# When TensorE reads the weight offsets of its blocks into registers

## The chip, the cores and the metric

The kernel runs on one core of one Trainium2 chip. The metric is the device time of one execution in microseconds (us), the median of several runs. A core has five engines that work side by side: TensorE (PE in the profile, with its weight loads shown apart as PEld), VectorE (DVE), ScalarE (ACT), GpSimd (POOL) and SyncE (SP), which here only issues DMA transfers. Each engine has a sequencer that takes its instructions in order, and a letter q behind the engine's name in the profile (PEldq, SPq) means an instruction of the sequencer.

## What is computed

An attention layer that picks chunks of keys, and behind it a mixture of experts. The second half is what matters here:

```python
def reference(**kwargs):
    attn_out = _attn_ref(q, k, v)                 # (4, 8, 768, 64)
    x = attn_out.transpose(0, 2, 1, 3).reshape(3072, 512)
    return _moe_ref(x, ...)

def _moe_ref(x, w_gate, w1_dense, w2_dense, w1, w2):
    h_dense = np.maximum(x @ w1_dense, 0.0)       # dense path, every token
    y_dense = h_dense @ w2_dense
    logits = x @ w_gate                           # 8 experts
    expert_idx = np.argmax(logits, axis=1)        # one expert for a token
    ...                                           # gate_w: its softmax weight
    for e in range(E):
        mask = expert_idx == e
        h = np.maximum(x[mask] @ w1[e], 0.0)
        y_moe[mask] = gate_w[mask, None] * (h @ w2[e])
    return y_dense + y_moe
```

Which tokens an expert gets is known only on the chip. So the kernel sorts the tokens by expert into a table in DRAM, and works through it in 31 blocks of 128 rows (24 full blocks' worth of tokens, and up to 7 more because each expert's last block may be partly filled). Each block belongs to one expert.

## The kernel before

There are 16 pairs of heads in four batches; a batch's gate, ranks and dense path are filled in between the attention work of the next batch. The last batch has no next one: its dense path lies between the first blocks of experts. All weights of the experts are in SBUF, in one tile. What tells one block's expert from another's is an offset along the columns of this tile. VectorE works the offsets out in two lists, one of the first N1 = 11 blocks, known before the last batch is routed, and one of the other N2 = 20. They are whole numbers in a row of one partition, `eo`; a second row `ro` says where a block's rows begin in the table.

```python
    N1 = (N * (B - 1) // B - E * 127 + 127) // 128
    N2 = NBLK - N1
...
    eo = const.tile([1, NBLK], mybir.dt.int32)
    ro = const.tile([1, NBLK], mybir.dt.int32)
    zo = const.tile([1, E], mybir.dt.int32)
...
        def lists(last, cnt):
            def row(name, n=E, dt=FP):
                return mg.tile([1, n], dt, name=f"{name}{last}", bufs=1)
            I32 = mybir.dt.int32
            n, i0 = (N2, N1) if last else (N1, 0)
            ...
            nc.vector.tensor_reduce(out=ef, in_=ge, op=ALU.add, axis=mybir.AxisListType.X)
            nc.vector.tensor_scalar(eo[:, i0 : i0 + n], ef, float(E - 1), float(2 * NK * 512), ALU.min, ALU.mult)
```

TensorE needs an offset in a register of its sequencer. The helper `registers` makes one read instruction for all values of a slice; `load_offs(n)` reads those up to block n that haven't been read yet. SyncE reads `ro` in the same way.

```python
    offs = []
    rows = []

    def registers(to, src, engine, n, top, why):
        k = len(to)
        _, v = nc.values_load_multi_w_load_instructions(src[:, k:n], engines=[engine], min_val=0, max_val=top,
                                                        skip_runtime_bounds_check_because=why)
        to.extend(v)

    def load_offs(n):
        registers(offs, eo, mybir.EngineType.PE, n, (E - 1) * 2 * NK * 512, "the expert of a block is at most the last")

    def load_rows(n):
        registers(rows, ro, mybir.EngineType.SP, n, EMPTY, "blocks lie in their expert's rows, or are the empty one")
```

In the last pair of heads, SyncE reads its first list and starts to fetch the first blocks' rows:

```python
            if p == NP - 1 and u == 5:
                load_rows(N1)
            if p == NP - 1 and u >= 5:
                fetch(u - 5)
```

Then come the blocks. `tx` transposes a block's rows on TensorE, VectorE copies them out of PSUM. `e1` is the first matmul with the expert's weights (four instructions, each at the block's offset plus a constant), ScalarE applies the relu. `th` transposes the result, ScalarE copies it. `e2` is the second matmul, VectorE multiplies by the token's gate weight, and GpSimd adds the rows to the output by an indirect DMA.

```python
        wef = we.rearrange("p e j f -> p (e j f)")
        def tx(i):
            s = es[i]
            tp = p1.tile([128, NK, 128], HF, name="tp", tag="tr")
            for ko in range(NK):
                nc.tensor.transpose(tp[:, ko], s["x"][:, ko * 128 : (ko + 1) * 128].bitcast(HF), ident)
            s["xT"] = xT = et.tile([128, NK, 128], HF, name="exT")
            nc.vector.tensor_copy(xT, tp)
...
        def e1(i):
            s = es[i]
            hp = p2.tile([128, 512], FP, name="hp", tag="h")
            for ko in range(NK):
                nc.tensor.matmul(hp, s["xT"][:, ko], wef[:, bass.ds(offs[i] + ko * 512, 512)],
                                 start=(ko == 0), stop=(ko == NK - 1))
            s["h"] = h = et.tile([128, 512], HF, name="eh")
            nc.scalar.activation(h, hp, AF.Relu)

        def th(i):
            s = es[i]
            tp = p1.tile([128, NK, 128], HF, name="tp", tag="tr")
            for j in range(NK):
                nc.tensor.transpose(tp[:, j], s["h"][:, j * 128 : (j + 1) * 128], ident)
            s["hT"] = hT = et.tile([128, NK, 128], HF, name="ehT")
            nc.scalar.copy(hT, tp)
...
        def e2(i):
            s = es[i]
            yp = p3.tile([128, Dm], FP, name="yp", tag="y")
            for j in range(NK):
                nc.tensor.matmul(yp, s["hT"][:, j], wef[:, bass.ds(offs[i] + (NK + j) * 512, 512)],
                                 start=(j == 0), stop=(j == NK - 1))
            o = et.tile([128, Dm], FP, name="yo", bufs=4)
            nc.vector.tensor_scalar(o, yp, s["x"][:, Dm : Dm + 2].bitcast(FP), None, ALU.mult)
            sc = nc.gpsimd.indirect_dma_start(
                out=out, out_offset=bass.IndirectOffsetOnAxis(ap=s["x"][:, Dm + 2 : Dm + 4].bitcast(mybir.dt.int32), axis=0),
                in_=o, in_offset=None, bounds_check=N - 1, oob_is_err=False, compute_op=ALU.add)
            apart(sc, "add", "every token is in one block")
```

The loop puts `e1` of a block, the transposes of the next, parts of the last batch's dense path (`extra`), `e2` of the block before and `th` of this one behind each other:

```python
        AHEAD = 8
        READY = 3
        load_offs(N1)
        tx(0)
        extra = {0: a[:NT] + [a[NT], ranks], 1: places, 2: [empty]}
        for n, f in enumerate(d):
            extra.setdefault(1 + n * (N1 - 2) // len(d), []).append(f)
        got = FIRST
        for i in range(NBLK):
            if i == READY:
                load_rows(NBLK)
            if i + 1 == N1:
                load_offs(NBLK)
            while got < min(i + AHEAD + 1, NBLK if i >= READY else N1):
                fetch(got)
                got += 1
            e1(i)
            if i + 1 < NBLK:
                tx(i + 1)
            for f in extra.get(i, ()):
                f()
            if i > 0:
                e2(i - 1)
            th(i)
        e2(NBLK - 1)
```

`load_offs(N1)` stands ahead of the first block, `load_offs(NBLK)` at the head of block 10.

Of the kernel before, what the change touches and what calls it, by code (L numbers as in the profile page):

```python
# [12 lines left out]
ALU = mybir.AluOpType  # L13
# [4 lines left out]
def kernel(  # L18
# [12 lines left out]
    nc = tc.nc  # L31
# [4 lines left out]
    E = 8  # L36
    F = 512
    NK = Dm // 128
# [4 lines left out]
    NBLK = NM + E - 1  # L43
# [3 lines left out]
    const = ctx.enter_context(tc.tile_pool(name="const", bufs=1))  # L47
# [5 lines left out]
    EMPTY = E * CAP  # L53
# [3 lines left out]
    N1 = (N * (B - 1) // B - E * 127 + 127) // 128  # L57
    N2 = NBLK - N1
# [100 lines left out]
    num = const.tile([128, NM, 1], mybir.dt.int32)  # L159
    zt = const.tile([128, XW], U16)  # L160
    used = const.tile([1, E + 1], FP)
    eo = const.tile([1, NBLK], mybir.dt.int32)
    ro = const.tile([1, NBLK], mybir.dt.int32)
    zo = const.tile([1, E], mybir.dt.int32)
    xbig = [const.tile([128, NT, XW], HF, name=f"xbig{i}") for i in range(2)]
# [87 lines left out]
    def batch_fills(b):  # L253
# [63 lines left out]
# [7 lines that stand above are left out]
            nb = row("nb", dt=I32)  # L324
            nc.vector.tensor_single_scalar(nb, cnt, 127.0 if last else 0.0, ALU.add)
            nc.vector.tensor_single_scalar(nb, nb, 7, ALU.arith_shift_right)
            nf = row("nf")
            if last:
                nc.vector.tensor_tensor(nf, nb, used[:, 0:E], ALU.subtract)  # L329
                nc.vector.tensor_tensor(zo, cnt, erow, ALU.add)  # L330
            else:
                nc.vector.tensor_copy(nf, nb)
            cum = row("cum")
            nc.vector.tensor_tensor_scan(cum, eone, nf, 0.0, ALU.mult, ALU.add)
            step = row("step")
            if last:
                nc.vector.tensor_tensor(step, used[:, 1 : E + 1], used[:, 0:E], ALU.subtract)
                nc.vector.tensor_tensor(step, step, nf, ALU.subtract)
                nc.vector.tensor_scalar(step, step, 128.0, float(CAP), ALU.mult, ALU.add)
            else:  # L340
                nc.vector.tensor_scalar(step, nf, -128.0, float(CAP), ALU.mult, ALU.add)
                left = row("left")
                nc.vector.tensor_tensor(left, nf, cum, ALU.subtract)
                nc.vector.tensor_single_scalar(left, left, float(N1), ALU.add)
                nc.vector.scalar_tensor_tensor(used[:, 0:E], left, 0.0, nf, ALU.max, ALU.min)
            ge = mg.tile([1, n, E], FP, name=f"ge{last}", bufs=1)
            nc.vector.tensor_tensor(ge, iob[:, 0:n].unsqueeze(2).to_broadcast([1, n, E]),
                                    cum.unsqueeze(1).to_broadcast([1, n, E]), ALU.is_ge)
            ef = row("ef", n)
            nc.vector.tensor_reduce(out=ef, in_=ge, op=ALU.add, axis=mybir.AxisListType.X)  # L350
            nc.vector.tensor_scalar(eo[:, i0 : i0 + n], ef, float(E - 1), float(2 * NK * 512), ALU.min, ALU.mult)
            nc.vector.tensor_tensor(ge, ge, step.unsqueeze(1).to_broadcast([1, n, E]), ALU.mult)
            rs = row("rs", n)
            nc.vector.tensor_reduce(out=rs, in_=ge, op=ALU.add, axis=mybir.AxisListType.X)
            nc.vector.scalar_tensor_tensor(rs, iob[:, 0:n], 128.0, rs, ALU.mult, ALU.add)
            if last:
                h0 = row("h0", 1)
                nc.vector.tensor_single_scalar(h0, used[:, 0:1], 128.0, ALU.mult)
                nc.vector.tensor_scalar(ro[:, i0 : i0 + n], rs, h0, float(EMPTY), ALU.add, ALU.min)
            else:  # L360
                nc.vector.tensor_copy(ro[:, 0:n], rs)
# [52 lines left out]
        at = {}  # L414
# [10 lines left out]
    offs = []  # L425
    rows = []

    def registers(to, src, engine, n, top, why):
        k = len(to)
        _, v = nc.values_load_multi_w_load_instructions(src[:, k:n], engines=[engine], min_val=0, max_val=top,  # L430
                                                        skip_runtime_bounds_check_because=why)
        to.extend(v)

    def load_offs(n):
        registers(offs, eo, mybir.EngineType.PE, n, (E - 1) * 2 * NK * 512, "the expert of a block is at most the last")

    def load_rows(n):
        registers(rows, ro, mybir.EngineType.SP, n, EMPTY, "blocks lie in their expert's rows, or are the empty one")

    es = [dict() for _ in range(NBLK)]  # L440

# [7 lines left out]
    with (  # L449
# [38 lines left out]
        def prep_kt(p):  # L488
            kp = st[p]["kp"]
            nc.vector.tensor_copy(kT[p % NB][0][0:64], kp[0:64])  # L490
            nc.vector.tensor_copy(kT[p % NB][1][64:128], kp[64:128])
# [121 lines left out]
        for i, (p, u) in enumerate(seq):  # L613
            n1 = p + 1 if p + 1 < NP else None
            n2 = p + 2 if p + 2 < NP else None
            if i + ahead_n < len(seq):
                scores(*seq[i + ahead_n])
            if u == 2 and n1 is not None:
                prep_s(n1)
            if u == 4 and n2 is not None:  # L620
                prep_k(n2)
            if u == 5 and n2 is not None:
                prep_q(n2)
            if u == 7 and n2 is not None:
                prep_kt(n2)
            if u == 9 and n2 is not None:
                prep_ub(n2)
            for f in fills.pop(i % (HP * NU) - LAG, ()):
                f()
            if i >= LAG:  # L630
                finish(*seq[i - LAG])
            if u == 0 and n2 is not None:
                cast_v(n2)
                load(p + 4, "v")
                if p == 1:
                    load_dense(st[n2]["cast"])
                if p == 2:
                    route_consts()
                for _ in range(2 if p >= 10 else 1):
                    if p > 1 and wq:  # L640
                        load_expert(*wq.pop(0), st[n2]["cast"])
            if u == 7:
                cast_qk(p + 3)
                load(p + 5, "kq")
            if p == NP - 1 and u == 5:
                load_rows(N1)
            if p == NP - 1 and u >= 5:
                fetch(u - 5)
        for i in range(len(seq) - LAG, len(seq)):
# [4 lines left out]
    with (  # L654
# [8 lines left out]
        a, d, ranks, places, _ = batch_fills(B - 1)  # L663
# [19 lines left out]
# [20 lines that stand above are left out]
            if i < N1:  # L703
                tc.declare_no_dep(sc.ins, group="dense", reason="the first blocks hold no token of the last batch")
                tc.add_to_no_dep_group("add1", sc.ins)
# [10 lines left out]

        AHEAD = 8
        READY = 3
        load_offs(N1)
        tx(0)  # L720
        extra = {0: a[:NT] + [a[NT], ranks], 1: places, 2: [empty]}
        for n, f in enumerate(d):
# [2 lines left out]
        for i in range(NBLK):  # L725
            if i == READY:
                load_rows(NBLK)
            if i + 1 == N1:
                load_offs(NBLK)
            while got < min(i + AHEAD + 1, NBLK if i >= READY else N1):  # L730
                fetch(got)
                got += 1
# [4 lines that stand above are left out]
                f()  # L737
            if i > 0:
                e2(i - 1)
            th(i)  # L740
        e2(NBLK - 1)

# [29 lines left out]
```

## Time and profile before

| | |
|---|---|
| device time, median of 3 runs | 298.36 us (296.98 to 298.44) |
| span of the profiled execution | 296.6 us |
| mean granted TensorE clock | 0.947 |
| TensorE busy | 232.7 us, 78% of the span |
| VectorE / ScalarE / GpSimd busy | 64% / 59% / 55% |
| attention ends, first transposes of a block | 188.8 us |
| first matmul of block 0 / of block 30 | 192.53 / 287.12 us |
| last scatter issued | 292.3 us |

The page has the span in 40 slices of 7.4 us; each digit is the busy share in tenths, PEclk the granted clock of TensorE in tenths:

```profile
PE   1179777797499988499998499598599819999991
PEclk9999999999789999989999989979799977999997
DMA  7999999989497999399999237404769981786781
```

The blocks of experts fill about the last 14 digits. In the row of TensorE there are dips at every batch's end, and a "1" among the blocks of experts. In a list of groups, a row has line, engine, operation, the tiles written and read, the count, the busy time and the mean of one in ns, and behind a second bar the idle time of the engine just before these instructions with what ended it. Reads into registers aren't counted as busy time; they show as idle time of the engine, or in a view of the tile that they read.

### The profile page before, as it was taken

Reading aid. Unit: us, or ns where it says so; the run is one execution under the profiler, and the core shown is the slowest. Engines: PE = TensorE matmul, PEld = TensorE weight load, DVE = VectorE, ACT = ScalarE, POOL = GpSimd, SP = SyncE. Lnnn points to the kernel's source line nnn. Section 1 sums busy time; section 2 is a strip of 40 time slices with the busy share of each in tenths; the row PEclk is TensorE's granted clock in tenths of the full one; section 3 lists DMA queues with packets and bytes.
Section 4 is the critical chain, followed back from the end, with each engine's and each line's share of the span. In section 5 each row is a group of like instructions: output and inputs, shape, how many; then the busy total and the mean of one; then the engine's idle time right before and its main releaser. Section 6 shows DMA issues by size and latency. Waiting matters only on the chain.

```text
span 296.6 us, 7417 instructions
## 1 busy us (share of the span) xinstructions
PE 232.7 (78%) x2595; PEld 151.9 (51%) x2595; DVE 189.0 (64%) x592; ACT 174.2 (59%) x325; POOL 162.5 (55%) x200
## 2 busy tenths in 40 slices
PE   1179777797499988499998499598599819999991
PEld 1056555575267666266676266364255405555550
DVE  6479899999368899469799652354343503555542
ACT  3639788875269996359895359333255403555550
POOL 7575855665645664845665522007644413767674
PEclk9999999999789999989999989979799977999997
DMA  7999999989497999399999237404769981786781
GB/s 196 272 256 229 161 237 217 221 226 194 151 169 210 249 215 225 120 189 194 178 232 196 96 94 198 106 2 173 161 110 218 240 175 20 123 155 105 97 123 14
DMA packets 75972, 50.04 MB, mean 169 GB/s; under 512 B 30112, under 2 KB 69024, under 8 KB 75936
## 3 DMA queue, kind: packets, MB, share of 16 engines
q1 hardware_dynamic: 60288, 30.58, 40.8%
q0 software_dynamic: 15648, 18.99, 39.4%
q8 instruction: 21, 0.34, 0.5%
q14 instruction: 15, 0.12, 0.1%
HBM read 41.96 MB, written 18.88 MB: 205 GB/s over the span
## 4 chain that ended last, share of the span: by engine, by line
PE 24%; issue 24%; POOL 19%; ACT 10%; DVE 9%; DMA 6%; SPq 3%; another core or an unknown queue 2%; POOLq 1%; ACTq 0%
POOL out_dram L699 15%; PE yp L391 5%; PE sp L539 5%; ACT ex L543 5%; PE hp L382 4%; DMA vf<-in_v_dram 3%; PE op L558 3%; PE pp L512 2%; SPq L92 2%; ACT hT L384 2%; POOL table L366 2%; PE pp L498 2%; ACT qp L501 2%; DMA qf<-in_q_dram 1%
## 5 line engine op out<-in xcount | busy, mean ns | idle before, releaser
L543 ACT ACTIVATE ex<-sp 128x512 f16<-128x512 f32 (+1 forms) x176 | 90.8, 603 | 17.5 <-PE sp L539 13.7
L539 PE MATMUL sp<-rT,kT 128*128 128x128 f16 (+3 forms) x384 | 64.9, 264 | 5.9 <-ACT ex L543 4.1
L699 POOL DMA_INDIRECT out_dram<-yo,xg x31 | 48.2, 1555 | 37.5 <-DVE yo L698 36.9
L545 POOL TENSOR_SCALAR_AFFINE_SELECT ex<-ex 128x512 f16<-128x512 f16 x48 | 32.1, 674 | 41.8 <-ACT ex L543 39.6
L558 PE MATMUL op<-v,ex 128*128 128x65 f16 x672 | 46.2, 196 | 2.7 <-POOL ex L545 1.6
L558 PEld LDWEIGHTS <-ex 128*128 128x128 f16 x672 | 36.4, 99 | 15.6 <-POOL ex L545 3.9
L678 PE MATMUL hp<-we,exT 128*128 x124 | 34.4, 399 | 9.8 <-issue 7.5
L366 POOL DMA_INDIRECT table<-xbig,slot x24 | 23.6, 984 | 28.0 <-DVE nf L329 15.4
L698 DVE TENSOR_SCALAR yo<-yp,xg 128x512 f32<-128x512 f32 x31 | 23.3, 750 | 22.2 <-PE yp L695 15.3
L695 PE MATMUL yp<-we,ehT 128*128 x124 | 33.5, 395 | 4.2 <-ACT ehT L689 4.2
L539 PEld LDWEIGHTS <-kT 128*128 128x128 f16 x384 | 29.6, 99 | 13.3 <-issue 9.6
L481 DVE TENSOR_REDUCE ks<-kp 128x24 f16<-128x768 f16 x32 | 29.2, 944 | 11.0 <-ACT kp L477 10.9
L391 PE MATMUL yp<-wd,hT 128*128 128x512 f16 x96 | 28.4, 418 | 9.0 <-ACT hT L384 7.9
L689 ACT COPY ehT<-tp 128x512 f16<-128x512 f16 x31 | 18.1, 585 | 27.8 <-PE tp L687 24.0
L681 ACT ACTIVATE eh<-hp 128x512 f16<-128x512 f32 x31 | 18.5, 597 | 24.9 <-PE hp L678 18.1
L382 PE MATMUL hp<-xT,wd 128*128 128x384 f16 x128 | 26.3, 325 | 7.0 <-issue 5.0
L672 DVE COPY exT<-tp 128x512 f16<-128x512 f16 x31 | 13.1, 423 | 27.6 <-PE tp L670 20.1
L384 ACT ACTIVATE hT<-hp 128x384 f16<-128x384 f32 x32 | 15.8, 493 | 21.0 <-remote 9.0
L678 PEld LDWEIGHTS <-exT 128*128 128x128 f16 x124 | 11.5, 103 | 17.7 <-issue 11.0
L477 ACT COPY kp<-pp 128x768 f16<-128x768 f16 x16 | 12.9, 807 | 10.8 <-PE pp L475 10.8
L469 POOL CAST v<-vf 128x768 f16<-128x768 f32 x16 | 13.2, 827 | 10.8 <-PE op L558 7.7
L518 DVE MAX8 m<-pp 128x8 f32<-128x8 f32 (+4 forms) x160 | 16.2, 167 | 4.6 <-PE pp L512 4.3
(126 smaller groups left out, 401.9 us busy)
## 6 DMA issues: line engine op xcount, KB each, us to landing
we<-in_moe_w_dram POOLq DMA_DIRECT2D x16, 512.0 KB
kf<-in_k_dram SPq DMA_DIRECT2D x32, 192.0 KB
qf<-in_q_dram SPq DMA_DIRECT2D x32, 192.0 KB
vf<-in_v_dram SPq DMA_DIRECT2D x32, 192.0 KB
out_dram<-ys SPq DMA_DIRECT2D x48, 128.0 KB
xg<-table SPq DMA_DIRECT2D x31, 132.0 KB
table<-zt SPq DMA_DIRECT2D x9, 132.0 KB
wd<-in_moe_w_dense_dram POOLq DMA_DIRECT2D x2, 512.0 KB
```

Source lines behind the costliest of these rows:

```text
L366: sc = nc.gpsimd.indirect_dma_start(out=table, out_offset=bass.IndirectOffsetOnAxis(ap=keep["slot"][:, t : t + 1], axis=0), in_=xbig[b % 2 ...
L382: nc.tensor.matmul(hp, wd[:, ko, j * 128 : (j + 1) * 128], xT[:, ko, g * G * 128 : (g + 1) * G * 128], start=(ko == 0), stop=(ko == NK - 1))
L391: nc.tensor.matmul(yp, hold["h"][:, j, i * 128 : (i + 1) * 128], wd[:, NK + j], start=(j == 0), stop=(j == NK - 1))
L481: nc.vector.tensor_reduce(out=ks[:, i], in_=kp.rearrange("d (c w) -> d c w", w=32), op=op, axis=mybir.AxisListType.X)
L539: nc.tensor.matmul(sp[:, o : o + w], kT[p % NB][g][:, kt * 128 : (kt + 1) * 128], rT[p % NB][g][:, a * 128 : z * 128], start=(o == 0), sto ...
L543: nc.scalar.activation(ex[:, 0:o], sp[:, 0:o], AF.Exp, scale=0.125)
L545: nc.gpsimd.affine_select(out=ex, in_=ex, compare_op=ALU.is_ge, fill=0.0, base=0, pattern=[[0, 4], [1, 2], [2, 64]], channel_multiplier=-1)
L558: nc.tensor.matmul(s["op", g][:, t * (D + 1) : (t + 1) * (D + 1)], ex[:, o : o + 128], v16[p % NB][:, g, kt, :], start=first, stop=(last_o ...
L678: nc.tensor.matmul(hp, s["xT"][:, ko], wef[:, bass.ds(offs[i] + ko * 512, 512)], start=(ko == 0), stop=(ko == NK - 1))
L695: nc.tensor.matmul(yp, s["hT"][:, j], wef[:, bass.ds(offs[i] + (NK + j) * 512, 512)], start=(j == 0), stop=(j == NK - 1))
L698: nc.vector.tensor_scalar(o, yp, s["x"][:, Dm : Dm + 2].bitcast(FP), None, ALU.mult)
L699: sc = nc.gpsimd.indirect_dma_start(out=out, out_offset=bass.IndirectOffsetOnAxis(ap=s["x"][:, Dm + 2 : Dm + 4].bitcast(mybir.dt.int32), a ...
```

## The change

The offsets are read four at a time. The first four are asked for during the last pair of heads, where SyncE reads its first list; the others in the loop, whenever fewer than four blocks' offsets lie ahead, between `e2` of the block before and `th` of the block. A read never crosses from the first list to the second. The second list begins at a column that is a multiple of four (12 in place of 11), so that each read of four begins at such a column; the first list has 11 values and is read as 4, 4 and 3. The purpose is that TensorE doesn't stop for a long read in one place. SyncE's reads of `ro` stay as they were.

```diff
--- before.py
+++ after.py
@@ -159,7 +159,9 @@
     num = const.tile([128, NM, 1], mybir.dt.int32)
     zt = const.tile([128, XW], U16)
     used = const.tile([1, E + 1], FP)
-    eo = const.tile([1, NBLK], mybir.dt.int32)
+
+    N1R = -(-N1 // 4) * 4
+    eo = const.tile([1, N1R + N2], mybir.dt.int32)
     ro = const.tile([1, NBLK], mybir.dt.int32)
     zo = const.tile([1, E], mybir.dt.int32)
     xbig = [const.tile([128, NT, XW], HF, name=f"xbig{i}") for i in range(2)]
@@ -348,7 +350,8 @@
                                     cum.unsqueeze(1).to_broadcast([1, n, E]), ALU.is_ge)
             ef = row("ef", n)
             nc.vector.tensor_reduce(out=ef, in_=ge, op=ALU.add, axis=mybir.AxisListType.X)
-            nc.vector.tensor_scalar(eo[:, i0 : i0 + n], ef, float(E - 1), float(2 * NK * 512), ALU.min, ALU.mult)
+            e0 = N1R if last else 0
+            nc.vector.tensor_scalar(eo[:, e0 : e0 + n], ef, float(E - 1), float(2 * NK * 512), ALU.min, ALU.mult)
             nc.vector.tensor_tensor(ge, ge, step.unsqueeze(1).to_broadcast([1, n, E]), ALU.mult)
             rs = row("rs", n)
             nc.vector.tensor_reduce(out=rs, in_=ge, op=ALU.add, axis=mybir.AxisListType.X)
@@ -425,17 +428,21 @@
     offs = []
     rows = []
 
-    def registers(to, src, engine, n, top, why):
-        k = len(to)
-        _, v = nc.values_load_multi_w_load_instructions(src[:, k:n], engines=[engine], min_val=0, max_val=top,
+    def registers(src, engine, top, why):
+        _, v = nc.values_load_multi_w_load_instructions(src, engines=[engine], min_val=0, max_val=top,
                                                         skip_runtime_bounds_check_because=why)
-        to.extend(v)
-
-    def load_offs(n):
-        registers(offs, eo, mybir.EngineType.PE, n, (E - 1) * 2 * NK * 512, "the expert of a block is at most the last")
+        return v
+
+    def load_offs():
+
+        k = len(offs)
+        n, c = (min(4, N1 - k), k) if k < N1 else (min(4, NBLK - k), k - N1 + N1R)
+        offs.extend(registers(eo[:, c : c + n], mybir.EngineType.PE, (E - 1) * 2 * NK * 512,
+                              "the expert of a block is at most the last"))
 
     def load_rows(n):
-        registers(rows, ro, mybir.EngineType.SP, n, EMPTY, "blocks lie in their expert's rows, or are the empty one")
+        rows.extend(registers(ro[:, len(rows) : n], mybir.EngineType.SP, EMPTY,
+                              "blocks lie in their expert's rows, or are the empty one"))
 
     es = [dict() for _ in range(NBLK)]
 
@@ -644,6 +651,7 @@
                 load(p + 5, "kq")
             if p == NP - 1 and u == 5:
                 load_rows(N1)
+                load_offs()
             if p == NP - 1 and u >= 5:
                 fetch(u - 5)
         for i in range(len(seq) - LAG, len(seq)):
@@ -716,7 +724,6 @@
 
         AHEAD = 8
         READY = 3
-        load_offs(N1)
         tx(0)
         extra = {0: a[:NT] + [a[NT], ranks], 1: places, 2: [empty]}
         for n, f in enumerate(d):
@@ -725,8 +732,6 @@
         for i in range(NBLK):
             if i == READY:
                 load_rows(NBLK)
-            if i + 1 == N1:
-                load_offs(NBLK)
             while got < min(i + AHEAD + 1, NBLK if i >= READY else N1):
                 fetch(got)
                 got += 1
@@ -737,6 +742,8 @@
                 f()
             if i > 0:
                 e2(i - 1)
+            if len(offs) < min(i + 4, NBLK):
+                load_offs()
             th(i)
         e2(NBLK - 1)
```

## The prediction

> **What bounds the kernel now, and the views read.** The change touches one kind of instruction, TensorE's read of offsets from a tile into registers. I read four views in this order: what the tile of offsets (eo) is read by, TensorE's own waits in the last third of the run, the timeline of TensorE round the two reads, and the busy times in stretches of time. The first is the view of the tile eo, with the columns engine, operation, count, shortest/median/longest in ns, first and last start in us; beside it the same view of the tiles ro and zo, which SyncE reads in the same way.
>
> ```profile
> L430 PEldq TENSOR_LOAD <-eo x2: 1691/4772/7852, 190.6 to 235.7; - x2
> L430 SPq TENSOR_LOAD <-ro x2: 1635/3972/6309, 167.0 to 212.2; - x2
> L709 SPq TENSOR_LOAD <-zo x1: 537/537/537, 200.7 to 200.7; - x1
> ```
>
> Two reads on TensorE: 11 values in 1.691 us at 190.6, and 20 values in 7.852 us at 235.7. On SyncE 11 values took 1.635, 20 took 6.309, and 8 took 0.537. The time isn't proportional to the count, and this is the number on which the sum hangs. Next the waits of TensorE from 186 us on (what waited, for whom, us in total, times, longest):
>
> ```profile
> PE hp L678 <- issue: 7.5, 1, 7.5
> PE yp L695 <- ACT ehT L689: 4.2, 2, 3.4
> PE hp L678 <- DMA out_dram<-ys: 2.3, 1, 2.3
> ```
>
> The first and the third are the first matmul after each read. "issue" says that no semaphore held it: the sequencer itself was busy. The 2.3 us carry the name of a DMA, but the read of 1.691 lies in that gap as well. The timeline of TensorE round the second read (start, us, what, times, idle before):
>
> ```profile
> 235.83 0.39 PE L687 MATMUL tp<-ident,eh 128*128 128x128 f16 x4
> 243.70 1.86 PE L678 MATMUL hp<-we,exT 128*128 x4 [7.49 <-issue]
> 245.36 0.63 PE L670 MATMUL tp<-ident,xg 128*128 128x128 f16 x4
> 245.78 1.91 PE L695 MATMUL yp<-we,ehT 128*128 x4
> 247.49 0.63 PE L687 MATMUL tp<-ident,eh 128*128 128x128 f16 x4
> 247.92 1.11 PE L678 MATMUL hp<-we,exT 128*128 x4
> ...
> 250.18 1.03 PE L678 MATMUL hp<-we,exT 128*128 x4
> ```
>
> After the hole four matmuls take 1.86 us where later ones take 1.03. The stretches of time round both reads say why (columns: busy us and count by engine, granted clock, DMA share, GB/s):
>
> ```profile
> 236.30:243.70 7.40, 0.00 (x0) 0.00 (x0) 0.48 (x1) 0.58 (x1) 1.68 (x2) 0.84 0.86 197
> 243.70:250.20 6.50, 6.50 (x33) 3.33 (x33) 1.65 (x4) 1.78 (x3) 1.25 (x1) 0.66 0.09 21
> 250.20:252.40 2.20, 2.20 (x20) 1.26 (x18) 1.20 (x3) 1.18 (x2) 1.53 (x2) 1.00 0.66 80
> 193.50:196.80 3.30, 3.30 (x22) 2.20 (x20) 1.70 (x4) 0.75 (x2) 0.00 (x0) 0.50 0.02 5
> ```
>
> The granted clock is 0.66 in the 6.5 us after the second hole, and 0.50 for 3.3 us soon after the first. In the third stretch TensorE is busy all the time, and blocks then start every 2.17 us (timeline: first matmuls at 250.18, 252.35, 254.52). So TensorE sets the end in the blocks of experts; the page's chain of waits names GpSimd's scatters ("POOL out_dram L699 15%"), but in that stretch each scatter idles some 0.6 us for its block's result, so it follows TensorE.
>
> [...] The trace doesn't agree with one figure for all: 0.067 us per value for the 8, 0.154 for the 11, 0.393 for the 20. [...] the trace shows some lead of the sequencer: the second read starts at 235.7, while the four transposes issued before it start at 235.83. [...] after 7.49 us of idling the trace has 0.66, and after the stop of 2.32 us, with 0.46 us of waiting just before, it has 0.50, so a shorter gap can also do it.
>
> **The change part by part.** With N1 = 11 and N2 = 20 the reads become 4, 4, 3 and then five of 4. The program's instruction order shows that the source line of a read doesn't decide its place: each stands just before the first matmul of the block that needs it first, that is before blocks 0, 4, 8, 11, 15, 19, 23 and 27, as the two old ones stood before 0 and 11. The second list of offsets starts at column 12 in place of 11, so every read of four begins at a multiple of 16 bytes.
>
> What a read costs. Reading the durations as groups of four values from a 16-byte boundary and single values otherwise: 8 values are two groups in 0.537, so 0.27 a group. The 11 are those two and three singles, (1.691 - 0.537) / 3 = 0.385 each. The 20 start at column 11, byte 44, which is no such boundary: 20 singles, 7.852 / 20 = 0.393 each. Two independent figures for a single agree within 2%, so I take this reading: a four costs 0.27 to 0.3, the three 3 x 0.385 = 1.15.
>
> What of a read stands on the path. In the steady loop the next matmul comes 0.22 us after the transposes start, so at 236.05; it came at 243.70, 7.65 late for a read of 7.85. So a read shows its time less 0.20 us, which the sequencer's lead hides. A four then costs about 0.1 us, the three 0.95.
>
> The second read goes (blocks 10 to 13): first matmuls at 233.88 and 250.18 are 16.30 apart where three blocks need 3 x 2.17 = 6.51. That is 9.8 us too long: 7.65 of hole and 2.1 of half clock. All of it goes.
>
> The first read: in the kernel before its seven semaphore waits stand between 189.9 and 190.5, behind three transposes of x that wait for VectorE until 189.88; in the new order those transposes come after the first block's matmuls. So the read can start at about 190.0 rather than 190.65 and end at 190.3 rather than 192.34; the first matmul comes at about 190.5 in place of 192.53. That is 2.0 less, and the three transposes then cost 0.2: 1.8 gained. The half clock from 193.5 to 196.8 held work that needs half of that at full clock, at most 1.65 us, and VectorE's four copies of 0.42 there would set 1.7 us; so up to 1.5 gained, if the shorter gap no longer throttles. I count 1.2.
>
> Added: six fours in the loop at 0.1, 0.6 us; the three before block 8, 0.95 us.
>
> Sum: -9.8 - 1.8 - 1.2 + 0.6 + 0.95 = -11.25 us. From 298.36 that is 287.1. In the removed hole the DMA engines drained what they had: DMA share 0.86 in it, and 0.09 after it. Without the hole, scatters and stores lie closer; I add 0.6 us for that: 287.7.
>
> **The rivals.** First, that a read of four isn't cheap: if the group is eight values or if every value costs 0.39, a four takes 1.55 and shows 1.35, six of them 8.1 with 0.95 for the three. The first read would still be short by seven values of the eleven only in the first case. The gain is then about 4 us, 294.5. For it: nobody here reads four. Against it: the 8 in 0.537, and the change's rounding of the second list to a multiple of four. [...]
>
> Second, that a transfer takes the place of the hole. Before the hole DMA is at nine tenths or more in two slices of the page; a scatter issued at 237.06 must land before the block four later may reuse the result tile. That leaves four blocks of 2.17 us, 8.7 us. In the steady stretch one scatter takes GpSimd 1.55 and can be followed by the next after 0.6, so it keeps up. The DMA share at this pace is 0.66 to 0.73, not full. If stores still delay the scatters for some blocks, 2 to 3 us come back: 290.
>
> Third, that GpSimd becomes the bound: 1.55 + about 0.3 between issues is 1.85 for a block against 2.17. It doesn't, at this pace.
>
> Fourth, the stop of 3.38 us on "ACT ehT L689" near 210 us. It lies just behind six scatters into the table, and nothing in the change removes it. It moves with the first phase, and it could grow or shrink by a microsecond or two.
>
> **Range and chances.** The removal of the 9.8 us is nearly certain. Open are the cost of a four [...], the half clock of the first phase (0 to 1.5) and the stop near 210. All well gives 285.5; dear fours and no gain of clock give 291.5. I predict 287.7, 285.5 to 291.5. Two per cent faster is 292.4, so faster by more than that has 0.94, within two per cent 0.05, slower 0.01.
>
> **What would show it.** The view of eo in the new trace must have eight reads, seven near 0.27 to 0.3 us and one near 1.15. The wait of 7.5 us on "issue" must be gone, with no idle time of TensorE over some 0.3 us before a block's first matmul in blocks 11 to 30 except the very last wait, and the granted clock 1.00 there. The first matmul of block 0 should come about 2 us earlier after the attention ends. I am wrong if fours take over 0.8 us, if the second read's place shows a wait on a DMA, or if blocks start more than 2.3 us apart between the reads.

## The result

| | before | after |
|---|---|---|
| median, us | 298.03 | 288.86 |
| runs, us | 296.98 to 298.44 (4) | 287.41 to 289.64 (4) |
| profiled span, us | 296.6 | 287.9 |
| mean granted clock of TensorE | 0.947 | 0.946 |

The ratio is 0.969 (95% interval 0.965 to 0.974): 9.2 us less. A few executions fall into a slower state (in the experiment e0 one of 276.26 us, where the others start at 271.74); times here and below are medians of all runs, ratios come from the faster runs alone, so that the two differ a little. The prediction had 287.7. The profiled execution after the change is the longest of its four (289.64). The views follow in the order in which the prediction read them.

The view of the tile eo after the change (engine, operation, count, shortest/median/longest in ns, first and last start in us):

```profile
L432 PEldq TENSOR_LOAD <-eo x8: 331/489/1177, 191.2 to 271.4; - x8
```

There are eight reads where there were two. Taken one by one they last, in us: 0.79 (block 0), 1.18 (block 4), 0.78 (the three values before block 8), then 0.33, 0.33, 0.63, 0.33 and 0.34. SyncE's two reads of rows, which the change leaves alone, are as long as before: the view of the tile ro has 1.64 us for 11 values and 6.30 for 20.

TensorE's waits from 186 us to the end (who waited, for whom, us in total, times, longest):

```profile
PE yp L703 <- ACT ehT L697: 3.5, 2, 2.7
PE hp L686 <- DVE exT L680: 1.9, 1, 1.9
PE yp L394 <- issue: 1.7, 1, 1.7
PE hp L686 <- issue: 0.5, 2, 0.3
PE hp L686 <- DVE yo L706: 0.5, 1, 0.5
```

The wait of 7.5 us on "issue" is gone. Of the reads, what the view still names is one of the two waits of 0.27 us on "issue" (before block 19; the other is before block 3, where no read stands), and under the name of VectorE's yo the 0.5 us of block 4, in whose gap the read of 1.18 us lies. The 1.9 us lie before the first matmul of block 0, and the read of 0.79 lies in them. The 1.7 and 2.7 of the 3.5 belong to the stop near 210 us, which the prediction said would stay.

The timeline of TensorE at three of the reads (start, us, what, times, idle before):

```profile
226.90 0.39 PE L695 MATMUL tp<-ident,eh 128*128 128x128 f16 x4
227.13 1.03 PE L686 MATMUL hp<-we,exT 128*128 x4
...
236.01 0.39 PE L695 MATMUL tp<-ident,eh 128*128 128x128 f16 x4
236.37 1.02 PE L686 MATMUL hp<-we,exT 128*128 x4
...
253.66 0.39 PE L695 MATMUL tp<-ident,eh 128*128 128x128 f16 x4
254.31 1.02 PE L686 MATMUL hp<-we,exT 128*128 x4 [0.27 <-issue]
```

Without a read the block's matmul starts 0.22 us after the transposes. The four of 0.33 us at 236.01 makes that 0.36, so it shows 0.14 us. The four of 0.63 makes it 0.65 and shows 0.43. Here a read shows its time less 0.20 us, as the long one had done. The three values before block 8 (226.90 to 227.13) show nothing: that read started at 226.08 and was over at 226.86, before the transposes began. What starts a read can be seen beside ScalarE's timeline: each of these starts 0.06 us after ScalarE has finished the relu of the block before (226.08 after 226.02, 235.84 after 235.78), for which the transposes ahead of the read wait. In the steady loop these transposes follow at once (236.01); before block 8 they start only at 226.90, behind matmuls of the dense layer and the block before.

The stretches of time (busy us and count by engine PE, PEld, DVE, ACT, POOL; granted clock; DMA share; GB/s) after the first read, round the stop near 210 us, and in the place of the old hole:

```profile
194.00:197.00 3.00, 3.00 (x52) 2.35 (x51) 2.20 (x7) 0.64 (x2) 0.00 (x0) 1.00 0.02 5
208.80:215.60 6.80, 5.26 (x19) 2.37 (x20) 2.20 (x4) 2.36 (x4) 3.06 (x2) 0.50 0.90 170
236.30:243.70 7.40, 7.40 (x54) 4.07 (x52) 4.20 (x7) 4.11 (x7) 3.73 (x4) 1.00 1.04 206
```

In the place of the hole TensorE is busy all the time at full clock, while the DMA engines are as full as they were in it (1.04 against 0.86). The half clock after the first read is gone (1.00 where it was 0.50). The half clock behind the stop near 210 us has become longer: 0.50 for 6.8 us (208.78 to 215.60), where the same 6.8 us had 0.75 before (0.50 from 210.54 to 213.95 alone). In both traces the changes of the clock lie multiples of 3.41 us apart (the last part), and this is one step more.

Where the 8.65 us between the two profiled spans come from, with stages cut at the first matmuls of blocks in the two timelines:

| stage | before | after | difference |
|---|---|---|---|
| up to the transposes of block 0 (attention) | 188.81 | 189.72 | +0.91 |
| from there to block 0's matmul (first read) | 3.72 | 2.49 | -1.23 |
| to block 0's second matmul (e2) | 7.40 | 5.95 | -1.45 |
| to block 4's first matmul | 13.33 | 14.46 | +1.13 |
| block 4 to block 10 | 20.61 | 21.43 | +0.82 |
| block 10 to block 13 (old hole) | 16.30 | 6.65 | -9.65 |
| block 13 to block 30 | 36.95 | 37.77 | +0.82 |
| block 30 to the end | 9.47 | 9.46 | 0.0 |

### The profile page after: what moved, and what is told of

The parts are those of the page before. It is cut to its first block, busy times and chain, and to the rows that moved or that the text cites. A ratio compares the mean times of both kernels' runs of the same rounds, so it can differ in the third digit from the quotient of the medians.

```text
span 287.9 us, 7422 instructions
## 1 busy us (share of the span) xinstructions
PE 232.7 (81%) x2595; PEld 152.3 (53%) x2595; DVE 189.4 (66%) x592; ACT 174.6 (61%) x325; POOL 162.8 (57%) x200
## 4 chain that ended last, share of the span: by engine, by line
PE 47%; ACT 14%; DVE 14%; POOL 10%; issue 8%; another core or an unknown queue 5%; POOLq 1%; DMA 1%; SPq 0%; ACTq 0%; DVEq 0%
POOL out_dram L707 9%; PE yp L394 8%; PE hp L385 8%; PE sp L546 7%; ACT ex L550 6%; PE hp L686 5%; PE yp L703 4%; PE op L565 4%; PE pp L519 3%; ACT qp L508 2%; DVE m L525 2%; DVE ks L488 2%; ACT hT L387 2%; PE pp L533 2%
## 5 line engine op out<-in xcount | busy, mean ns | idle before, releaser
L703 PE MATMUL yp<-we,ehT 128*128 x124 | 32.6, 387 | 3.5 <-ACT ehT L697 3.5
L686 PE MATMUL hp<-we,exT 128*128 x124 | 33.0, 386 | 2.9 <-DVE exT L680 1.9
L385 PE MATMUL hp<-xT,wd 128*128 128x384 f16 x128 | 27.8, 340 | 7.8 <-ACT hT L387 4.8
L385 PEld LDWEIGHTS <-wd 128*128 128x128 f16 x128 | 12.2, 100 | 14.6 <-issue 10.4
L394 PEld LDWEIGHTS <-hT 128*128 128x128 f16 x96 | 9.4, 103 | 18.5 <-issue 13.2
```

Source lines behind the costliest of these rows:

```text
L385: nc.tensor.matmul(hp, wd[:, ko, j * 128 : (j + 1) * 128], xT[:, ko, g * G * 128 : (g + 1) * G * 128], start=(ko == 0), stop=(ko == NK - 1))
L394: nc.tensor.matmul(yp, hold["h"][:, j, i * 128 : (i + 1) * 128], wd[:, NK + j], start=(j == 0), stop=(j == NK - 1))
```

## The experiments

Three questions were open. Does a read's time come from the number of values, from where the list starts, or from the load on the DMA engines? Does it matter where in TensorE's stream the reads stand? And do SyncE's reads, as long as before, cost anything? The runs were on two other chips, e1 to e4 on one and the rest on the other. There the kernel before takes 286 us; no profile of it was taken there. In the profiles of the other runs TensorE doesn't stop for 3 us and more between blocks 0 and 4 (stage "to block 4" 7.6 us, not 13.3), and attention ends 9 to 13 us earlier (but in e5 at 188.9). The times in the expectations of e1 to e4 are meant for the first chip. Runs are compared with the kernel before as ratios, and with one another by stages.

### e5: the cost of a read by itself

After the last block, where the other engines have no work left, reads of several lengths and starts from a tile of zeros, each followed by a matmul that uses its last value. The kernel's own time says nothing.

```
+ SIZES = [(0, n) for n in (1,2,3,4,5,6,7,8,11,12,16,20)] + [(1,4),(2,4),(3,4),(4,4),(4,8),(11,4),(11,20),(12,20)]
+ for c, n in SIZES + SIZES:
+     _, at_ = nc.values_load_multi_w_load_instructions(mt[:, c : c + n], engines=[PE], ...)
+     nc.tensor.matmul(hp[:, 0:128], ident, wef[:, bass.ds(at_[n - 1], 128)], start=True, stop=True)
```

> The changed kernel, and behind its last block forty reads of a row of zeros on TensorE, each followed by one small matmul at the offset read: 1, 2, 3, 4, 5, 6, 7, 8, 11, 12, 16 and 20 values from byte 0, four values from bytes 4, 8, 12, 16 and 44, eight from byte 16, twenty from bytes 44 and 48, all of it twice. Its own time says nothing. Theory (groups of four from a 16-byte boundary): 0.27 to 0.33 us for each whole group, about 0.25 for each single value: 4 values 0.3, 8 values 0.55, 11 values 1.3, 12 values 0.8, 20 values 1.4 from byte 48 and 5 from byte 44, four values 1.0 from bytes 4, 8, 12 and 44. Rival (only whole groups of eight are fast): 4 values 1.0 from any byte, 12 values 1.55. Rival (cost grows with length squared, alignment is nothing): 20 values the same from bytes 44 and 48.

Five of the reads in the view of the tile mt, in this order: 4 and 11 values from byte 0, 4 from byte 4, 20 from byte 44, 20 from byte 48 (the three figures are one duration in ns):

```profile
L755 PEldq TENSOR_LOAD <-mt x1: 339/339/339, 278.5 to 278.5; - x1
...
L755 PEldq TENSOR_LOAD <-mt x1: 1315/1315/1315, 283.0 to 283.0; - x1
L755 PEldq TENSOR_LOAD <-mt x1: 1007/1007/1007, 289.1 to 289.1; - x1
L755 PEldq TENSOR_LOAD <-mt x1: 4747/4747/4747, 295.4 to 295.4; - x1
L755 PEldq TENSOR_LOAD <-mt x1: 1362/1362/1362, 300.4 to 300.4; - x1
```

All of them, in us (the second pass agrees within 2%; transfers were still under way in the first three reads, with a DMA share of 0.92, 0.58 and 0.11):

| values from byte 0 | 1 | 2 | 3 | 4 | 5 | 6 | 7 | 8 | 11 | 12 | 16 | 20 |
|---|---|---|---|---|---|---|---|---|---|---|---|---|
| us | 0.306 | 0.546 | 0.767 | 0.339 | 0.606 | 0.826 | 1.052 | 0.593 | 1.315 | 0.852 | 1.109 | 1.363 |

Four values from byte 4, 8 or 12 take 1.00 to 1.01, from byte 16 0.338, from byte 44 1.012. So the time of the reads that start at a multiple of 16 bytes (0, 16 and 48) goes by fours: 0.34 for the first and 0.256 for each further one, and each value left over costs about 0.24 ((1.315 - 0.593) / 3). The time of those with another start goes value by value to the end: 1.00 / 4 = 0.25 on average for four, and 4.747 / 20 = 0.237 for the twenty. Three cost more than twice as much as four. Neither the count alone nor the load on DMA explains this: one column of start makes 4.75 or 1.36 of the same 20 values, with a DMA share of 0.00 in the stretch of the longer one.

In the kernel the same read can be longer: 4.75 us quiet against 7.85 in the kernel before and 8.44 in e4 below, under a DMA share of 0.90 and 0.96, which is 1.65 to 1.78 times as long. But a full DMA doesn't always stretch a read: the aligned four before block 11 after the change took 0.33 us under a share of 0.90, and two unaligned fours of e2 (below) took 1.00 both under 0.97 and under 0.09. What stretches some reads is not shown.

### e1: the long read, started at column 12

Two reads of 11 and 20 as in the kernel before, and the second list at column 12.

```
-        n, c = (min(4, N1 - k), k) if k < N1 else (min(4, NBLK - k), k - N1 + N1R)
+        n, c = (N1, 0) if k < N1 else (N2, N1R)
         (the calls stand where the kernel before has them)
```

> Two reads as in the kernel before (11 values ahead of block 0, 20 ahead of block 11), and only the second list is moved from column 11 to column 12. Theory (groups of four from a 16-byte boundary, single values otherwise): the read of 20 takes five groups, 5 x 0.27 to 0.33 = 1.4 to 1.7 us in place of 7.85, the hole before block 11 is 1.2 to 1.5 us, the clock stays at 1.00 there, and the time is some 8.3 us below that of the kernel before: about 290. The read of 11 stays at 1.7. Rival (a read's cost grows faster than its length, and splitting it is what helps): the read of 20 stays near 7.8 us and the time near 298.

Measured: 279.22 us against 285.92, ratio 0.974 (0.968 to 0.979). The stretches in the read and behind it:

```profile
221.94:225.35 3.41, 1.01 (x8) 0.54 (x7) 0.93 (x2) 0.77 (x2) 2.58 (x2) 1.00 0.97 237
225.35:228.76 3.41, 3.41 (x12) 1.46 (x11) 0.42 (x1) 0.60 (x1) 0.00 (x0) 0.50 1.05 247
```

By the view of the tile eo the same 20 values in one read take 2.77 us where they took 7.85. But TensorE idles 2.40 us, and then works 3.4 us at half clock: stage 10 to 13 takes 10.76 against the 6.51 of three undisturbed blocks, 4.25 too many. The theory holds for the alignment; its 1.4 to 1.7 us for the read and its full clock behind it don't.

### e2: reads by four, from column 11

The changed kernel with the second list at column 11, so that no four of it is aligned.

```
-    N1R = -(-N1 // 4) * 4
+    N1R = N1
```

> The changed kernel with the second list back at column 11, so its five reads of four begin at bytes 44, 60, 76, 92 and 108. Theory (alignment): each takes 4 x 0.26 to 0.39 = 1.0 to 1.6 us instead of 0.33, shows that less 0.2, and five of them cost 3 to 6 us more than in the changed kernel: 292 to 295. Rival (splitting alone helps, alignment doesn't matter): reads of 0.33, time as the changed kernel's, 288.9.

Measured: 278.86 us, ratio 0.974 (0.969 to 0.979), as e1. The waits of TensorE from 180 to 270 us that belong to the reads, and the stretches in and behind the longest read:

```profile
PE hp L686 <- DVE yo L706: 3.4, 4, 1.3
...
PE hp L686 <- issue: 2.3, 1, 2.3
```

```profile
218.35:221.76 3.41, 1.99 (x16) 1.07 (x14) 1.55 (x3) 1.68 (x3) 2.27 (x3) 1.00 1.01 195
221.76:225.17 3.41, 2.58 (x18) 1.42 (x18) 0.85 (x2) 0.75 (x2) 0.97 (x1) 1.00 1.10 223
```

By the view of the tile eo the five fours take 2.62, 1.68, 1.00, 1.00 and 1.23 us, 7.53 together. 5.70 of it is idle time of TensorE: 2.26 under "issue", the other four under VectorE's name (3.4). Counted from matmul to matmul as above, 6.5 shows, each read's time less 0.20, and that is all by which this run's 20 blocks are too long. In the timeline VectorE's yo had long been done by then; the read that stands in the same gap came last. Here no half clock follows (1.00). The stages from block 10 to 30 set the versions of the second list side by side: 53.63 us with neither (e4 below), 49.96 split only (e2), 47.71 aligned only (e1), 44.94 with both (e0 below, on the other chip; 44.41 on the first); 20 undisturbed blocks would take 43.46. Each part alone leaves a cost that the other takes away.

### e4: only the first list changed

The first list by fours, the second in one read from column 11.

```
-    N1R = -(-N1 // 4) * 4
+    N1R = N1
-        n, c = (min(4, N1 - k), k) if k < N1 else (min(4, NBLK - k), k - N1 + N1R)
+        n, c = (min(4, N1 - k), k) if k < N1 else (N2, N1)
```

> One half of the change alone: the first list by fours (4, 4, 3), the second as in the kernel before, 20 values from column 11 in one read. Theory: the read of 20 takes 7.5 to 7.9 us again and is followed by half clock; what is left of the gain is the first phase's, 1.2 us of shorter wait and up to 1.4 of clock, less the reads before blocks 4 and 8: 295.5 to 297. Rival (the first phase gives nothing that lasts, as the stop near 210 us takes it back): 298.

Measured: 282.0 us, ratio 0.986 (0.983 to 0.989). In the waits of TensorE from 180 to 270 us the hole stands at its full size:

```profile
PE hp L686 <- issue: 8.1, 1, 8.1
```

Stage 10 to 13 takes 16.68 us, as in the kernel before (16.30); the phase up to e2 of block 0 takes 8.44 (2.49 + 5.95) as in the changed kernel. So the two parts act apart from one another, and the first is worth 1.4% on this chip.

### e0: the changed kernel, on the chip of e5, e6 and e7

No edit.

> The changed kernel itself, timed beside the others on the same chip. The first ratio was 0.969; where the kernel before takes about 286 us, this is 277. The five reads of the second list take 0.33 to 0.7 us each and show that less 0.2.

Measured: 272.73 us against 286.10, ratio 0.958 (0.951 to 0.966). The first phase takes 8.45 us and stage 10 to 13 7.47, much as on the first chip (8.44 and 6.65). The gain is larger, 4.2% for 3.1%; the first chip's longer stop near 210 us is some of it, and the rest can't be placed without a profile of the kernel before on this chip. One of the waits here led to the last experiments. The longest of TensorE's waits from 176 to 262 us, and SyncE's timeline before it:

```profile
PE yp L703 <- ACT ys L238: 2.6, 1, 2.6
```

```profile
195.23 1.40 SPq L721 DMA_DIRECT2D table<-zt  x3
204.93 0.35 SPq L451 DMA_DIRECT2D xg<-table  x1
205.37 1.13 SPq L400 DMA_DIRECT2D out_dram<-ys  x2
```

SyncE issues nothing from 196.63 to 204.93. In that gap lies its read of 20 rows, from the tile ro:

```profile
L432 SPq TENSOR_LOAD <-ro x2: 1620/4802/7984, 159.1 to 196.7; - x2
```

The stores of ys queue behind the read (the first is issued at 205.37). ys has three buffers, so ScalarE's next copy into ys waits for a store ("ACT ys L238", idle 3.21 us for the DMA), its copy ehT waits behind that, and TensorE's second matmul, 2.59 us idle, behind both.

### e3: reads where the source has them

In all kernels so far each read is moved to just before the first matmul that needs it. Here TensorE's stay where the source calls them.

```
-                                                        skip_runtime_bounds_check_because=why)
+                                                        skip_runtime_bounds_check_because=why,
+                                                        bass_reorder=engine != mybir.EngineType.PE)
```

> The changed kernel with TensorE's reads kept where the source puts them: those of the first list in the last pair of heads, the five of the second list between the second matmul and the transposes of a block. Theory (the read's place decides what shows, here it lies in the time in which the sequencer would wait for ScalarE anyway): no idle time from the five reads, 0.85 us less than in the changed kernel from block 13 on, and the first matmul of block 0 comes some 0.9 us sooner after the attention: 287 to 287.5. Rival (the read costs the same wherever it stands): 288.9.

Measured: 273.92 us against 285.92, ratio 0.954 (0.949 to 0.959), not told apart from e0's 0.958 on the other chip. The two longest of TensorE's waits from 176 to 262 us:

```profile
PE yp L704 <- ACT ys L238: 5.0, 1, 5.0
PE hp L687 <- DVE xbig L577: 1.0, 1, 1.0
```

The trace has all three reads of the first list inside attention (at 164.0, 176.3 and 177.3), two of them earlier than the source calls them, and the five of the second list where the source has them. The wait before block 0's matmul falls from 1.9 to 1.0 us, and names what remains: VectorE's normalisation of the last heads (xbig). Its stage falls from 2.49 to 1.60. In the loop nothing is gained in sum, 37.46 us from block 13 to 30 for 37.47 in e0, but the place does matter: the read now stands ahead of the transposes that wait for ScalarE, and some 0.5 us of it are hidden in place of 0.20. A four of 0.33 us costs nothing. Those of 0.83 and 0.75 us cost 0.30 and 0.22; e0's four had 0.33 to 0.35. So the rival (the same cost wherever it stands) fails, and longer reads took back what the place gave. This profile is of a run 2.4 us above the median; e6 below, with its reads in the same places, shows the same (0.98 us cost 0.50, and 0.33 and 0.49 nothing). The stop on "ACT ys" is here 5.0 us, behind a read of rows of 9.4 us on SyncE.

### e7: the rows at column 12 as well

The changed kernel, with SyncE's second list of rows at column 12.

```
-    ro = const.tile([1, NBLK], mybir.dt.int32)
+    ro = const.tile([1, N1R + N2], mybir.dt.int32)
-                nc.vector.tensor_scalar(ro[:, i0 : i0 + n], rs, ...)
+                nc.vector.tensor_scalar(ro[:, e0 : e0 + n], rs, ...)
-        rows.extend(registers(ro[:, len(rows) : n], ...))
+        k = len(rows)
+        c = N1R if k else 0
+        rows.extend(registers(ro[:, c : c + n - k], ...))
```

> The changed kernel, and SyncE's second list of rows moved from column 11 to column 12 as well. Theory: SyncE's read of 20 falls from 7 to 9 us to 1.4 to 3, the output stores that queue behind it leave some 5 us sooner, ScalarE and VectorE get their result tiles back, and TensorE's stop on "ACT ys" of 2 to 5 us near block 6 to 8 goes with its half clock: 2 to 5 us below the changed kernel. Rival (the stop comes from the DMA engines being full, not from SyncE's queue): the stop stays, and the time is that of the changed kernel.

Measured: 270.63 us, ratio 0.950 (0.944 to 0.955). Its slowest run, 271.44, is below the fastest of e0, 271.74, on the same chip. The view of the tile ro, and all of TensorE's waits from 176 to 262 us:

```profile
L432 SPq TENSOR_LOAD <-ro x2: 1627/2378/3129, 161.0 to 198.7; - x2
```

```profile
PE hp L688 <- DVE exT L682: 1.9, 1, 1.9
PE hp L688 <- DVE yo L708: 0.6, 1, 0.6
PE yp L394 <- DVE ys L236: 0.2, 1, 0.2
```

The read falls from 7.98 to 3.13 us, the stop on "ACT ys" is gone, and stage 4 to 10 falls from 23.51 to 20.77. The DMA engines are as full as before there (203 to 215 us: 1.06, and 0.96 in e0), so the rival, full DMA engines, fails. This is the chain of e0 taken apart at its first link, and by the ratios it beats the changed kernel by some 0.8% (0.950 for 0.958). The 0.6 us under VectorE's name is again a read of offsets: the three values before block 8 took 1.63 us here and made the block 0.78 late, behind the same dense matmuls that hid them before.

### e6: e3 and e7 together

> Reads of TensorE kept in their place in the source, and SyncE's second list of rows at column 12: the two together. Theory: both gains add up, 0.86 s of nothing lost between them, about 2 us from the place and 2 to 5 from the rows below the changed kernel: ratio to the kernel before 0.935 to 0.955. Rival (both take away the same stop): no more than the better of the two.

(The 0.86 in its text has no meaning.) Measured: 271.64 us, ratio 0.949 (0.942 to 0.956): no different from e7. The first phase is 0.9 us shorter, but the loop from block 13 takes 39.32 against 37.61. The waits of all engines from 215 to 262 us name why:

```profile
POOL out_dram L710 <- DMA xg<-table: 7.0, 2, 6.7
...
DVE yo L709 <- DMA out_dram<-yo,xg: 3.5, 1, 3.5
```

A scatter waited 6.7 us for a transfer, VectorE's yo 3.5 us for a scatter's landing, and TensorE 1.9 us behind that. This is the prediction's second rival, in a version that it wasn't written for: once the reads are short, DMA may be the next bound. It is one profile, and the median doesn't resolve it.

## Why the prediction came out right, point by point

**The second read goes, -9.8.** Measured -9.65, and -9.79 without the 0.14 that the four before block 11 adds. e4 leaves this read alone and keeps the stage at 16.68. The step holds in size and cause.

**What a read costs.** The reading in groups of four from a 16-byte boundary was the author's estimate from three durations (0.537, 1.691 and 7.852 us); it holds (e5). The numbers were close by way of an error: 0.27 for a four was the mean of two groups in one read, where the first costs 0.34 and the next 0.256, and that read was SyncE's (0.537; TensorE's eight take 0.593). The 0.385 and 0.393 for a single value were taken as its price, and are the price in these two reads, under a DMA share of 0.67 and 0.90; the quiet one is 0.24. That the two agreed was no proof of it. Of the seven fours, four took 0.33 to 0.34; 0.63, 0.79 and 1.18 were not foreseen, and the last is above the 0.8 us that the prediction named as a sign of being wrong, a limit that no trace had given.

**What of it shows, time less 0.20.** Confirmed at every four in the steady loop. Six fours at 0.1 were to be 0.6; they came to 0.69 before block 4 (1.10 us from the transposes to the matmul, at half clock, where the kernel before had 0.41), 0.14 before block 11 and 0.82 from block 13 to 30, 1.65 together. The term was too small because a four is 0.33 and not 0.27 to 0.3, and because two of the six were longer (1.18 and 0.63 us). The three before block 8 were to cost 0.95 and cost 0: it took 0.78 and lay wholly under earlier matmuls, since the lead of 0.20 us is one of the steady loop and not of the blocks with dense matmuls between them. That the two errors cancel, 1.65 against 1.55, is luck.

**The first read, -1.8 and -1.2.** Measured -1.23 and -1.45. The first is the term that was mis-sized. Counted from the transposes of block 0, the read was to start after 1.2 us and the matmul to follow after 1.7; they came after 1.51 and 2.49. Two things were missed. The read starts only when VectorE has finished the normalisation of the last heads (xbig, until 191.19; the read starts at 191.23): 0.3 us. And this four took 0.79 us and not 0.3: 0.5 us. It takes 0.79 at this place in e0, e2, e4 and e7 too, and 0.53 in e5; why is not shown. With no read there (e3), 1.0 us of waiting remain, under the name of the normalisation. The half clock went as hoped (1.00 from 194 to 197 us), and brought a little more than counted.

**The stop near 210 us** was left in, at no change. Its waits are 4.4 us (2.7 and 1.7), but the half clock behind it lasts 6.8 us in place of 3.4. The rest of two stages lies round it, 1.13 - 0.69 = 0.44 to block 4 (block 3 already starts 0.43 us late) and 0.82 to block 10: 1.3 us that the sum didn't have. In the profile several engines stand idle there at once (VectorE 5.58 us up to 207.68, ScalarE 3.10 up to 206.24 and 2.42 up to 209.15), beside and after six scatters into the table (199.07 to 206.37). Stops of over 3 us in this stage weren't there on the other chips, and nothing was tried on their cause; it stays open. The smaller stop that e0 and e3 have some blocks later is another one, and e7 removes it.

**The 0.6 us for closer transfers**, and the second rival. Scatters did run late, as the rival said. GpSimd's timeline (start, us, what, idle before):

```profile
239.73 1.57 POOL L707 DMA_INDIRECT out_dram<-yo,xg  x1 [0.93 <-DMA xg<-table]
243.41 1.56 POOL L707 DMA_INDIRECT out_dram<-yo,xg  x1 [2.11 <-DMA xg<-table]
245.27 1.55 POOL L707 DMA_INDIRECT out_dram<-yo,xg  x1 [0.30 <-issue]
...
254.88 1.55 POOL L707 DMA_INDIRECT out_dram<-yo,xg  x1 [0.62 <-DVE yo L706]
```

The scatter at 243.41 is 2.0 us behind its block's result (ready at 241.44). From there GpSimd needs 1.86 us for one where TensorE needs 2.17 for a block, and by 254.88 it waits for results again. TensorE never waited for it, so 0.6 should have been 0. The third rival's 1.85 for a scatter was right too, and GpSimd is no bound here.

**The first rival**, a dear four, fails at 0.33 us in the steady loop. It would have held without the alignment: e2's fours take 1.0 to 2.6.

The parts measured, -9.79 - 1.23 - 1.45 + 1.65 + 0.44 + 0.82, and 0.91 by which attention ended later in this execution, which the change doesn't touch, sum to -8.65. The prediction had -10.65. Of the 2.0 between them the stop makes 1.3 and attention 0.9; the first phase gives 0.3 less than counted and the reads left cost 0.1 more, and the transfers take 0.6 less. So the mechanism was right where the gain lies, in the second read, and the closeness of the whole owes something to errors of both signs. The stop was among the rivals, as one that could move by a microsecond or two; attention was in no step.

## What to carry to other kernels

Start a list that a sequencer reads into registers at a multiple of 16 bytes and make its parts multiples of four values: here one column of padding gave 5.9 us of the second list's 8.7, splitting alone 3.7, and only both together removed the hole (stages of e1, e2, e4 and e0). Then look at the same read on every other engine: SyncE computes nothing here, but in e0 its read of 7.98 us held up the stores queued behind it, and through their buffers TensorE for 2.59 us; with the read at 3.13 us that stop was gone (e7). When a read must stay, try it where the engine still has issued work to do while its sequencer would only wait: ahead of the transposes that wait for ScalarE 0.5 us were hidden (e3, e6), behind them 0.20.

## What the runs showed of the hardware

- In e5 a register read that started at byte 0, 16 or 48 took 0.34 us for the first four values and 0.256 for each further four; from bytes 4, 8, 12 and 44 it took 0.24 to 0.25 for each value. Under a DMA share of 0.9 to 1.0 the same 20 values took 1.65 to 2.0 times as long (7.85 and 8.44 against 4.75; 2.77 against 1.36), but fours under such a share took their quiet time (0.33; 1.00 unaligned).
- In the traces before and after the change the granted clock changes only at times that are multiples of 3.41 us apart (before: 0.50 from 193.47 to 196.88, 210.54 to 213.95 and 241.26 to 248.09; after: from 208.78 to 215.60). The length of a hole alone didn't decide whether half clock followed: after 2.40 us of idling in e1 the clock was 0.50, after 2.26 us in e2 it stayed 1.00, and so it did after 3.01 us in e4. What differs is how the idling lies in the stretches of 3.41 us: e1's 2.40 us lie in one (221.94 to 225.35), while e2's are cut into 1.42 and 0.83 at 221.76, and e4's into 1.50 and 1.51 at 212.03. The gap before block 0 fits: 2.32 us in one stretch before the change, at most 1.56 in one after it. In the two traces each of the 13 stretches in which TensorE idled 2.09 us or more was followed by half clock; of those with 1.63 us or less, five were too (0.89 to 1.24; three of the five had half clock themselves), so this isn't the whole of it. For the holes of 2 to 3 us named here, half clock came or stayed away with where the stretches happened to lie.
- In the steady loop of the changed kernel the read before block 11 started 0.06 us after ScalarE's relu of block 10 (235.84 after 235.78), and the matmul followed 0.19 us after the read's end (236.18, matmul at 236.37). How much of a read was hidden differed with what lay ahead of it: 0.20 us in the steady loop, some 0.5 with the read ahead of the transposes (e3, e6), and 0.85 where a dense matmul lay between (e7: 1.63 us, of which 0.78 showed).
